# Strassen's seven products for the second matmul, one batch behind, with the attention of batch 1 inside the first stream

## The chip, the cores and the metric

The kernel runs on one core of a Trainium2 chip. Times are microseconds (us) on the device, the median of several executions; each execution is put in a state by its time and by the clock granted to TensorE, and only runs of the fast state are compared. All runs quoted here were of the fast state. PE is TensorE (the matmul engine), PEld its weight loads, PSUM the memory in which its matmuls accumulate, DVE is VectorE, ACT is ScalarE, POOL is GpSimd, SP is SyncE, which here issues transfers.

## The reference, cut to what matters

```
B, H, S, D = 8, 12, 448, 64
scores = q @ k.T / sqrt(64) - log(448)          # per batch and head
x = sigmoid(scores) @ v                         # heads side by side: [3584, 768]
h = x @ w_in                                    # [3584, 2048], the "first GEMM"
out = (h * sigmoid(h)) @ w_out                  # [3584, 768],  the "second GEMM"
```

Inputs and output are 32-bit floats; the kernel multiplies in 16 bits.

## The kernel before

A batch has 448 rows, which are 7 blocks of 64. Matmuls use the array in quarters: four of 64x64 run at once. The kernel is a stream: for each batch 8 pairs of column tiles of the first GEMM, then the output tiles of the second, and between them steps of the next batch's attention (21 per batch: one score with its sigmoid, and one piece of the values). An output tile is two blocks of rows by 768 columns:

```python
def o_pair(units):                      # units: (tile, column half), two of them
    ...
    yield from products(
        "o", NFC, lhs,                  # NFC = 16 slices of 128 of the inner size 2048
        lambda u, k: w_out_sb[:, k, units[u][1] * NO2 : (units[u][1] + 1) * NO2],
        lambda u: po[:, u, :NO2],       # NO2 = 384
    )
    ... # one or two evictions on VectorE with a scale, and the stores

def tiles_of(b):                        # 3 or 4 output tiles after the pairs of batch b
    return range((R * b) // 2, (R * (b + 1)) // 2)
```

Queries and keys come in by rows and have to be transposed. Of batch 1 the second and third thirds of the heads are transposed on PE, inside the stream of batch 0; later batches use DMA transposes:

```python
for kind, share, b in stream:
    ...
    if kind == "h":                                 # a pair of the first GEMM
        if share == 0.5:
            attend()
        if b == 0 and pairs in (2, 5) and 0.9 < share < 1:
            i = 1 if pairs == 2 else 2
            transpose_pe(1, i, "qk", pool=ps_sc, tag="pssc")
            if i == 1:
                cast(1, 2, "q", nc.vector)
                cast(1, 2, "k", nc.gpsimd)
```

The stream of batch 0 ends with three output tiles, so attention of batch 1 is spread over pairs and tiles.

## Time and profile before

The time is 392.29 us (392.22 to 394.06). I cut the execution at the first matmul of the first GEMM of each batch, as PE's timeline shows it; "tail" is batch 7 to the end of the span.

| stretch of the kernel before | us |
|---|---|
| prologue (loads, attention of batch 0) | 28.13 |
| stage 0 | 46.69 |
| stage 1 | 49.27 |
| stages 2 to 6 together | 222.98 |
| tail | 43.31 |
| span | 390.38 |

PE is busy 98% of the span and runs at its peak rate in the steady stages; the lines that carry this are in the prediction (the 2.4 GHz in it is that of the formula of the page that it cites under (1)).

### The profile page before, as it was taken

The numbers are of one execution on the slowest core, as the hardware profiler recorded it, in microseconds if no ns is written. First come the engines' busy times: TensorE is split into PE (matmuls) and PEld (weight loads), VectorE is DVE, ScalarE is ACT, GpSimd is POOL, SyncE is SP. The second block draws the span as 40 slices with busy tenths as digits, with TensorE's granted clock in tenths as the row PEclk, the third lists the DMA queues.
The fourth block names the chain that finished last, engine by engine and source line by source line (L and its number), as shares of the span: only waits on it lengthen the run. The fifth ranks groups of instructions, "written<-read, shape, count | busy, mean of one in ns | idle before, by whom it ended". The sixth has DMA issues, their size and how long they took to land.

```text
span 390.4 us, 16893 instructions
## 1 busy us (share of the span) xinstructions
PE 381.4 (98%) x7944; PEld 296.8 (76%) x7944; DVE 135.2 (35%) x142; ACT 226.7 (58%) x234; POOL 55.2 (14%) x69
## 2 busy tenths in 40 slices
PE   8999999999999999999999999999999999999995
PEld 4665688788888777877788777877788777877785
DVE  3443542234222442144322333234420433324312
ACT  3986576566644776567644777667745677633200
POOL 4622102120300111013100121002100000000000
PEclk9999999999999999999999999999999999999999
DMA  8999997999993767687572875667673100130033
GB/s 289 231 241 243 179 180 158 177 235 251 228 158 64 202 131 161 113 202 150 144 119 54 208 144 143 125 122 202 151 118 83 44 3 2 44 83 1 2 83 82
DMA packets 64998, 54.18 MB, mean 139 GB/s; under 512 B 35488, under 2 KB 61472, under 8 KB 64928
## 3 DMA queue, kind: packets, MB, share of 16 engines
q1 hardware_dynamic: 50768, 40.64, 44.0%
q0 software_dynamic: 13632, 11.80, 20.2%
q8 instruction: 62, 1.02, 1.1%
q10 hardware_dynamic: 528, 0.66, 0.6%
q14 instruction: 8, 0.07, 0.0%
HBM read 45.61 MB, written 11.01 MB: 145 GB/s over the span
## 4 chain that ended last, share of the span: by engine, by line
PE 90%; DMA 6%; DVE 1%; issue 1%; POOL 1%; ACT 0%; SPq 0%; POOLq 0%
DMA v_1_461<-in_v_dram 4%; DMA stk_0_219<-in_k_dram 2%; PE po_0_2_1_1696 L236 1%; PE po_0_24_1_8966 L258 1%; PE po_0_3_1_2401 L236 1%; PE po_0_5_1_2758 L236 1%; PE po_0_12_1_5062 L236 1%; PE po_0_26_1_9104 L258 1%; PE po_0_25_1_9035 L258 1%; PE po_0_23_1_8578 L236 1%; PE po_0_22_1_8391 L236 1%; PE po_0_17_1_7009 L236 1%; PE po_0_8_1_3813 L236 1%; PE po_0_20_1_7531 L236 1%; PE po_0_19_1_7366 L236 1%; PE po_0_18_1_7192 L236 1%
## 5 line engine op out<-in xcount | busy, mean ns | idle before, releaser
L236 PEld LDWEIGHTS <-w_in_sb 64*64 64x64 f16 x2688 | 95.6, 107 | 32.7 <-ACTq L249 7.9
L236 PEld LDWEIGHTS <-gT_712 64*64 64x64 f16 x448 | 18.8, 107 | 3.0 <-issue 0.2
L236 PEld LDWEIGHTS <-gT_5400 64*64 64x64 f16 x448 | 18.2, 107 | 3.4 <-ACTq L249 0.2
L236 PEld LDWEIGHTS <-gT_3096 64*64 64x64 f16 x448 | 18.2, 107 | 3.4 <-ACTq L249 0.2
L236 PEld LDWEIGHTS <-gT_1877 64*64 64x64 f16 x448 | 18.5, 107 | 1.6 <-ACTq L249 0.5
L236 PEld LDWEIGHTS <-gT_6485 64*64 64x64 f16 x448 | 17.2, 107 | 2.5 <-ACTq L249 0.5
L236 PEld LDWEIGHTS <-gT_4181 64*64 64x64 f16 x448 | 17.2, 107 | 2.5 <-ACTq L249 0.5
L258 PEld LDWEIGHTS <-w_in_sb 128*64 128x64 f16 x192 | 12.5, 110 | 5.8 <-issue 0.3
L236 PEld LDWEIGHTS <-gT_7700 64*64 64x64 f16 x384 | 13.7, 107 | 2.5 <-ACTq L249 0.2
L258 PEld LDWEIGHTS <-gT_8740 128*64 128x64 f16 x160 | 12.4, 110 | 1.6
L92 PEld LDWEIGHTS <-zeros 64*64 64x64 f16 x192 | 6.6, 120 | 5.2 <-issue 2.2
L236 PE MATMUL po_0_1_0_1293<-w_out_sb,gT_712 64*64 64x384 f16 x128 | 6.5, 323 | 0.0
L236 PE MATMUL po_0_3_1_2401<-w_out_sb,gT_712 64*64 64x384 f16 x64 | 6.4, 323 | 0.0
L236 PE MATMUL po_0_3_1_2401<-w_out_sb,gT_1877 64*64 64x384 f16 x64 | 6.4, 323 | 0.0
L236 PE MATMUL po_0_21_1_8206<-w_out_sb,gT_7700 64*64 64x384 f16 x128 | 6.4, 323 | 0.0
L236 PE MATMUL po_0_7_1_3620<-w_out_sb,gT_3096 64*64 64x384 f16 x128 | 6.4, 323 | 0.0
L236 PE MATMUL po_0_14_1_5924<-w_out_sb,gT_5400 64*64 64x384 f16 x128 | 6.4, 323 | 0.0
L236 PE MATMUL po_0_2_1_1696<-w_out_sb,gT_712 64*64 64x384 f16 x128 | 6.3, 324 | 0.0
L236 PE MATMUL po_0_15_1_6117<-w_out_sb,gT_5400 64*64 64x384 f16 x128 | 6.2, 323 | 0.0
L236 PE MATMUL po_1_1_1_1480<-w_out_sb,gT_712 64*64 64x384 f16 x128 | 6.2, 323 | 0.0
L236 PE MATMUL po_0_8_1_3813<-w_out_sb,gT_3096 64*64 64x384 f16 x128 | 6.2, 323 | 0.0
L236 PE MATMUL po_0_22_1_8391<-w_out_sb,gT_7700 64*64 64x384 f16 x128 | 6.2, 323 | 0.0
(783 smaller groups left out, 934.2 us busy)
## 6 DMA issues: line engine op xcount, KB each, us to landing
w_in_sb<-in_moe_w_in_dram POOLq DMA_DIRECT2D x8, 384.0 KB, 10.5
w_out_sb<-in_moe_w_out_dram POOLq DMA_DIRECT2D x2, 1536.0 KB, 17.1
v_0_142<-in_v_dram POOLq DMA_DIRECT2D x3, 224.0 KB, 6.1
v_1_461<-in_v_dram POOLq DMA_DIRECT2D x1, 672.0 KB, 14.0
v_2_1551<-in_v_dram POOLq DMA_DIRECT2D x1, 672.0 KB, 9.1
v_3_2037<-in_v_dram POOLq DMA_DIRECT2D x1, 672.0 KB, 8.4
v_4_3256<-in_v_dram POOLq DMA_DIRECT2D x1, 672.0 KB, 6.8
v_5_4341<-in_v_dram POOLq DMA_DIRECT2D x1, 672.0 KB, 6.3
```

The costliest lines, as they stand in the source:

```text
L92: nc.tensor.matmul(pz[half(t), j, :S], zeros[half(j), :D], zeros[half(j)], start=True, stop=True)
L236: mm = nc.tensor.matmul(out_of(u)[half(c)], lhs(u, k, c)[half(row)], rhs(u, k)[half(row)], start=(ph == 0 and k == 0), stop=(ph == 1 and k ...
L258: nc.tensor.matmul(out_of(u)[half(c)], lhs(u, k, c), rhs(u, k), start=(k == 0), stop=(k == nk - 1),)
```

## The change

Intent: fewer matmuls. Eight blocks of rows are taken together as a 2x2 arrangement (two halves of rows, two halves of the inner size), the output weights as 2x2 too, and Strassen's method makes the four result quarters from seven products instead of eight. Its sums of activations and weights go to VectorE. As 56 blocks are seven groups of eight, the second GEMM starts only after batch 1's pairs and runs one batch behind; stage 0 has no output tile left, and all of batch 1's attention lies within its eight pairs and behind them. The diff, cut to its core:

```diff
-            if b == 0 and pairs in (2, 5) and 0.9 < share < 1:
-                ...                      # batch 1's transposes on PE, in the stream
-                transpose_pe(1, i, "qk", pool=ps_sc, tag="pssc")
...
+    for nm in "qk":                      # end of the prologue, behind the loads of batch 1
+        transpose_dma(1, 1, nm)
...
+            if n == 1:                   # n: step of batch 1's attention
+                load_w_in(3)
+                load_v(1)                # the load of it in the prologue stays as well
+            if n == 3:
+                cast(1, 2, "q", nc.vector)
+                cast(1, 2, "k", nc.gpsimd)
+                for nm in "qk":
+                    transpose_dma(1, 2, nm)
+            if n == 14:
+                load_v(2)
+                load_w_out()             # was at steps 4 and 6
...
-            gs = list(tiles_of(b))
-            ... # 3 or 4 tiles of o_pair
+                if b == 1 and f2 >= 4:
+                    sum_w(f2 - 4)        # half a sum of the output weights
+            if b > 0:
+                for s in o_group(b):
+                    yield *s, b
...
+    def o_group(b):                      # x, y: two accumulators in PSUM
+        sum_g(1)
+        ...                              # for batch 1 two half sums of weights, two more below
+        yield from mm(x, of_g(0, 0), w11)
+        p1 = keep(x, "p1", "part1")
+        sum_g(2)
+        yield from mm(y, of_g(0, 1), w21)
+        halves(y, osb[0][:, :, lo], p1)
+        sum_g(4)
+        yield from mm(x, of_s(2), t_sums[2], start=False)   # adds to the product that was kept
+        u2 = keep(x, "u2", "part1")
+        sum_g(3)
+        yield from mm(y, of_s(1), t_sums[1])
+        p5 = keep(y, "p5", "part2")
+        yield from mm(x, of_s(3), t_sums[3], start=False)
+        halves(x, osb[1][:, :, hi], p5)
+        yield from mm(y, of_s(4), w22, start=False)
+        halves(y, osb[0][:, :, hi], u2)
+        yield from mm(x, of_g(1, 1), t_sums[4], start=False)
+        halves(x, osb[1][:, :, lo])
+        ...                              # the stores, here and between the products
```

## The prediction

> **What bounds the kernel now.** I read the page first (busy shares, slices), then the chain of work that ended last, then the timeline of PE at the borders of the stages, then the waits, the timelines of ACT and POOL and the DMA issues.
>
> Page, parts 1 and 2:
>
> ```profile
> PE 381.4 (98%) x7944; PEld 296.8 (76%) x7944; DVE 135.2 (35%) x142; ACT 226.7 (58%) x234; POOL 55.2 (14%) x69
> ...
> PE   8999999999999999999999999999999999999995
> ...
> DMA  8999997999993767687572875667673100130033
> ```
>
> PE has work all the time, no other engine is near its limit over the whole, but the DMA engines are full for the first 13 slices of 9.76 us. A busy PE is not yet a PE at its peak, so I looked at the rate, in the chain in order of time:
>
> ```profile
> 18.69 14.00 DMA v_1_461<-in_v_dram
> ...
> 129.63 1.14 PE ph_2_3220 L236 x24
> ...
> 157.16 1.30 PE po_0_8_1_3813 L236 x32
> ...
> 370.83 5.20 PE po_0_25_1_9035 L258 x64
> ```
>
> 24 matmuls of 64x64x448 take 1.14 us (47.4 ns each), 32 of 64x64x384 take 1.30 us (40.6 ns each), 64 of the full-height form take 5.20 us (81 ns). With four quadrants working at once 448 columns at 2.4 GHz are 46.7 ns: the PE runs at its peak. So in the steady part time is the number of matmuls. Where the stages lie (the first matmul of the first GEMM of batches 0, 1, 2, 3, 6, 7), in the timeline of PE:
>
> ```profile
> 28.13 0.95 PE L236 MATMUL ph_0_713<-xT_414,w_in_sb 64*64 64x448 f16 x16
> ...
> 74.82 1.01 PE L236 MATMUL ph_0_1878<-xT_1262,w_in_sb 64*64 64x448 f16 x16
> ...
> 124.09 0.97 PE L236 MATMUL ph_0_3097<-xT_2367,w_in_sb 64*64 64x448 f16 x16
> ...
> 166.84 0.95 PE L236 MATMUL ph_0_4182<-xT_3586,w_in_sb 64*64 64x448 f16 x16
> ...
> 304.39 0.95 PE L236 MATMUL ph_0_7701<-xT_6975,w_in_sb 64*64 64x448 f16 x16
> ...
> 347.07 0.38 PE L258 MATMUL ph_0_8741<-xT_8176,w_in_sb 128*64 128x448 f16 x2
> ```
>
> So: prologue 28.1, stage 0 46.7, stage 1 49.3, stages 2 to 6 together 223.0 (alternately 42.7 and 47.4, for three or four output tiles), tail 43.3; in all 390.4, and the measured time is 1.9 above the span.
>
> **What the Trainium skill says.** (1) "TensorE: Matmul & The Clock Gate", section "Back-to-back issue gap": about N/2.4 + 2.5 ns per warm matmul. The trace agrees: 81 ns for two column tiles of 384, half of 162.5. (2) "VectorE: DVE Perf Modes", "The perf-mode tier table": tensor_tensor on 16-bit SBUF operands runs at 2x (1224 ns for 2048 elements), at 1x with a PSUM operand. The trace has only PSUM forms: 896 elements in 1.09 us. (3) "PSUM — Partial Sum Buffer", "The four PSUM rules": a matmul without the first flag accumulates, and reads by VectorE don't change that; so the change may read a partial sum, store it and go on adding. No run yet shows it. (4) "DMA: Bandwidth & Descriptors", "Queues, rings and completion order": each DMA engine takes turns between queues packet by packet, so 256-byte packets of a transpose beside 1 KB packets of a load get a small share of the bytes. The trace agrees in part (rivals, below).
>
> **The change part by part.**
> *Removed from PE.* The second GEMM now makes seven products of (4 blocks of 64 rows) x 1024 x 384 for every 8 blocks, where eight were made. Before: 24 tiles of 128 quarter matmuls and the equal of 4 tiles at the end (5.20 us each); after: six groups of 448 and a last one of 7 x 32 full-height ones. 384 x 40.6 ns = 15.6 us, and 20.8 - 18.2 = 2.6 us in the tail: 18.2 us. The four PE transposes of batch 1 (56 short matmuls, about 2.3 us seen as longer pairs 2 and 5 of stage 0) become DMA transposes.
> *Where it falls.* A stage of batches 1 to 6 now has 8 row blocks for the work of 7, so it isn't shorter than before: 8 pairs of the first GEMM at 2.65 (one attention step in each) = 21.2; 448 x 40.6 ns = 18.2; 13 attention steps x 8 x 47.4 ns = 4.9; allowance for hand-overs 0.5; sum 44.8, against a mean of 44.6 before. The gain is that stage 0 loses its three output tiles (15.6 us) and stage 1 and the tail half a tile each.
> *Added to DVE.* Per group four sums of 2048 elements, about 1.2 us each by (2), and seven evictions where 3.5 were, 0.95 us each:
>
> ```profile
> 370.87 0.96 DVE L305 TENSOR_SCALAR osb_8965<-po_0_24_1_8966 128x768 f32<-128x768 f32 x1 [3.21 <-PE po_0_24_1_8966 L258]
> ```
>
> About 8 us more per group, 56 us in all, and 8 sums of weights (7 us once). Inside a group a product with its two attention steps takes 64 x 40.6 + 2 x 379 = 3.36 us, and DVE has one eviction, one sum and at times an eviction of attention, 2.2 to 3.2 us. It keeps up. Critical is product 3: its sum waits for the eviction of product 1, 0.2 + 0.95 + 1.2 = 2.35 us after product 1's end, and product 2 covers 3.36. So on the path nothing, but in the tail, without attention, a product takes 2.6 us and DVE also about 2.6 (its sums are split in two there): I allow 1.2 us of stalls.
> *Row change-overs.* The order of instructions shows 14 instead of 7 per two batches. They cost nothing where an attention step lies between the halves, and the new places (every 8 steps) are such.
> *Stage 0.* Its 21 scores now all have to lie within eight pairs. PE: two scores and 48 matmuls = 2.65, with less attention to cover the row change-over: 2.8. ACT needs two score sigmoids at a spacing of 0.89 and one of the GEMM:
>
> ```profile
> 24.46 1.05 ACT L191 ACTIVATE attnT_2_520<-psc_2_4_614,bias_s 128x896 f16<-128x896 f32 x1
> 25.35 1.06 ACT L191 ACTIVATE attnT_2_520<-psc_2_5_633,bias_s 128x896 f16<-128x896 f32 x1
> ```
>
> 2.6 us, just below. So 8 x 2.8 + 0.3 = 22.7. Then four scores, all 21 value steps and the next batch's first score, 26 pieces of 4 matmuls at 0.19 us = 4.9; and the value accumulator has one buffer, so it waits for its eviction twice (1.3 each), 0.7 for a PSUM slot that the seventh pair's multiply frees, 0.4 at the end: 8.6. With a wait for the transposes of 5.5 (first rival): 36.8.
> *Sum.* 28.1 + 36.8 + stage 1 (44.8 + 1.8 for the arrival of the output weights and the sums of weights) 46.6 + 5 x 44.8 = 224.0 + tail (18.4 + 18.2 + 1.2 + 4.2 from the last matmul to the end, 3.9 before) 42.0 = 377.5; plus 1.9 = 379.4 us, 3.3% below.
>
> **Rivals.**
> *A. Stage 0 waits for DMA.* The order of instructions shows that batch 1's values are loaded twice (the old load stays, and a second one is added behind the last input weights), and that the transposes of its second third of heads stand in their queue behind the load of its last third:
>
> ```profile
> 37.50 0.93 POOL L148 CAST xk_2_929<-stk_2_653 128x896 f16<-128x896 f32 x1 [7.26 <-DMA stk_2_653<-in_k_dram]
> ...
> stk_2_653<-in_k_dram SPq DMA_DIRECT2D x1, 448.0 KB, 10.5
> ...
> w_out_sb<-in_moe_w_out_dram POOLq DMA_DIRECT2D x2, 1536.0 KB, 17.1
> ```
>
> That load lands at 37.4, the transposes come behind it while the weights and the second value load (0.69 MB at about 0.19 MB per us, estimate 3.6 us) keep the engines full until about 44. Scores need them at about 38. Later in the trace a transpose alone moves 204 GB/s (last column), and the next one, as a value load sets in beside it, far less:
>
> ```profile
> 64.00:65.00 1.00, 1.00 (x29) 0.74 (x24) 0.57 (x1) 0.49 (x2) 0.63 (x1) 1.00 1.05 204
> 65.00:66.00 1.00, 1.00 (x34) 0.89 (x28) 0.00 (x0) 0.81 (x1) 0.00 (x0) 1.00 0.67 39
> ```
>
> So the wait is 0 to 9 us; I took 5.5. Without it the time is 374; at 9, 383.
> *B. The output weights come late.* They are asked for near the end of stage 0 instead of at 38 us, need 17 us alone, and share the engines with batch 2's loads. The sums of weights are wanted about 22 to 25 us later and stand in DVE's order before multiplies that free PSUM. For: the same 0.19 MB per us. Against: two pairs of slack. It would make 379 into 382 to 385.
> *C. DVE becomes the bound inside the groups* (sums at 1x, 2.2 us each, or held up by casts on POOL). A product would then be 3.5 to 4.3 us instead of 3.36: 7 x 7 x 0.5 = 25 us, all gain gone, 395 or more. Against: the skill's table and a DVE share of about 52%. I give it 5%.
>
> **Range and chances.** Steady stages are well known (each 0.3 us there makes 1.5 us); stage 0's wait has a width of 9 us, stage 1's 4, the tail's 2. That gives 373 to 386. The limit of 2% is 384.5, reached only if A and B are both bad, or by C: faster 0.82, within 0.16, slower 0.02.
>
> **What would show it.** Stage borders in PE's timeline: stages 2 to 6 at 44.8 each (over 46 says C), stage 0 at 36.8 (31 says that no wait for transposes happened), tail 42.0. Sums of 2048 elements at 1.2 us. The waits of PE list the scores of batch 1 behind a DMA, and DVE's first sum of weights behind the output weights. Matmuls fall by 504. Wrong would be: PE idle inside the groups behind DVE, or a stage 0 that takes no time for transposes.

## The result, and the profile after

The changed kernel takes 387.56 us (386.62 to 389.35, 4 runs) against 392.43 of the kernel before in the same rounds: ratio 0.9872, 95% interval 0.9825 to 0.992, which at the 2% limit is "same". The time lies above the predicted range. (Ratios here are the mean time of one kernel's fast runs over that of the other's of the same rounds, so not quite the ratio of the medians that I quote.)

The page after: PE's busy time and matmuls, then PE, PE's clock and DMA in 40 slices, here of 9.66 us:

```profile
PE 360.9 (93%) x7440; PEld 272.8 (71%) x7440; DVE 195.4 (51%) x213; ACT 225.6 (58%) x234; POOL 58.9 (15%) x70
...
PE   7999079799899999999999999999999999999995
...
PEclk9999669999999999999999999999999999999999
DMA  8999968999999959199642975568760600032005
```

There are 504 matmuls fewer, as intended, and PE is busy 20.5 us less. But slice 5 (38.6 to 48.3 us) has PE at 0, and there and in the next slice the clock is at six tenths. Before, no slice of PE was below 8 except the last, and the clock row was all nines. The first matmuls of batches 0, 1, 2 and 7 in PE's timeline (start, duration, then what it is):

```profile
28.58 0.39 PE L251 MATMUL ph_0_741<-xT_428,w_in_sb 64*64 64x448 f16 x4
...
74.44 0.39 PE L251 MATMUL ph_0_1464<-xT_1369,w_in_sb 64*64 64x448 f16 x4
...
122.07 0.35 PE L251 MATMUL ph_0_2663<-xT_1970,w_in_sb 64*64 64x448 f16 x1
...
345.06 0.38 PE L275 MATMUL ph_0_8554<-xT_7892,w_in_sb 128*64 128x448 f16 x2
```

| stretch | before | predicted | after | miss |
|---|---|---|---|---|
| prologue | 28.13 | 28.1 | 28.58 | +0.5 |
| stage 0 | 46.69 | 36.8 | 45.86 | **+9.1** |
| stage 1 | 49.27 | 46.6 | 47.64 | +1.0 |
| stages 2 to 6 | 222.98 | 224.0 | 222.99 | -1.0 |
| tail | 43.31 | 42.0 | 41.41 | -0.6 |
| span | 390.38 | 377.5 | 386.48 | +9.0 |

The whole miss is stage 0. In the view of waits, the longest of PE, and in the chain of work that ended last, in order of time, what stands around it:

```profile
PE psc_1_0_981 L197 <- DMA kT_1_701<-xk_1_631: 11.7, 1, 11.7
```

```profile
31.62 19.20 DMA kT_1_701<-xk_1_631
50.82 0.04 issue
50.87 0.59 PE psc_1_0_981 L197 x3
51.45 2.24 PE ph_3_954 L251 x18
53.69 0.40 PE psc_1_1_1012 L197 x3
```

kT_1 is the transposed keys of batch 1's second third. Their transfer is issued at 31.62 and lands at 50.82; the first score that reads them waits 11.7 us. After it PE is slow. Table by windows (width, busy time of PE, PEld, DVE, ACT, POOL with counts, the granted clock, DMA share, GB/s):

```profile
41.50:42.00 0.50, 0.00 (x0) 0.00 (x0) 0.00 (x0) 0.00 (x0) 0.00 (x0) 1.00 0.24 16
...
42.50:43.00 0.50, 0.00 (x0) 0.00 (x0) 0.00 (x0) 0.00 (x0) 0.00 (x0) 0.50 1.23 198
...
55.00:55.50 0.50, 0.50 (x12) 0.31 (x8) 0.00 (x0) 0.50 (x2) 0.00 (x0) 0.50 0.00 0
...
56.00:57.00 1.00, 1.00 (x28) 0.53 (x24) 1.00 (x1) 0.69 (x1) 0.00 (x0) 1.00 0.64 82
```

PE stops at 39.2; at 42 the clock falls to half, and it comes back only between 55.5 and 56, some 5 us after PE has started again. The Trainium skill, "TensorE: Matmul & The Clock Gate", section "What's actually happening", puts the fall to half after an idle window of about 3.4 us and the return after about 3.4 us of sustained work, with a window that runs freely, so that the moment varies by 0.5 us. The trace has 2.8 us and about 4.8 us; other kernels of this study spread more widely (closing list).

Why is the transfer late? The DMA view of three stretches: the software queue carries the loads issued by POOL, the hardware queue those issued by SP, the transposes among them (packets, MB, share). First the changed kernel from 37.4, when batch 1's last load has landed, to 51:

```profile
q0 software_dynamic: 1654, 1.54, 74.3%
q1 hardware_dynamic: 2723, 0.67, 54.6%
```

then, within it, from 38 to 42 and from 42 to 46:

```profile
q0 software_dynamic: 466, 0.46, 90.4%
q1 hardware_dynamic: 474, 0.12, 46.8%
```

```profile
q0 software_dynamic: 644, 0.60, 89.2%
q1 hardware_dynamic: 638, 0.16, 30.3%
```

and from 50.9 to 51.9, after the software queue has run dry:

```profile
q1 hardware_dynamic: 910, 0.22, 116.0%
```

While both have work the two queues advance packet for packet (466 and 474, 644 and 638), though a load's packet is about 1 KB and a transpose's 256 bytes. Four transposes wait in the queue, 896 packets each; the keys are the second, so 1792 packets have to pass. From 38 to 46 they pass at 139 per us (1112 in 8 us), alone at 910. About 1.1 of these 8 us are a stall of both queues, from 41.0 to 42.1 (the table above has 16 GB/s at 41.5 and 198 at 42.5); by their packets experiments 2, 4, 5, 10 and 12 have one too, between 40 and 43, and its cause is open. Outside it the transposes pass at about 150 to 170 per us. This is the turn-taking that the prediction quoted from the skill, seen here in counts. It slows the loads as well: outside the stall they move 0.15 MB per us, where the prediction reckoned with 0.19.

### The profile page after: what moved, and what is told of

It is laid out like the page before. It is cut to its first block, busy times and chain, and to the rows that moved or that the text cites. A ratio compares the mean times of both kernels' runs of the same rounds, so it can differ in the third digit from the quotient of the medians.

```text
span 386.5 us, 16052 instructions
## 1 busy us (share of the span) xinstructions
PE 360.9 (93%) x7440; PEld 272.8 (71%) x7440; DVE 195.4 (51%) x213; ACT 225.6 (58%) x234; POOL 58.9 (15%) x70
## 3 DMA queue, kind: packets, MB, share of 16 engines
q10 hardware_dynamic: 768, 1.25, 0.9%
## 4 chain that ended last, share of the span: by engine, by line
PE 73%; DMA 15%; DVE 6%; ACT 4%; issue 1%; SPq 0%; POOL 0%; DVEq 0%; POOLq 0%
DMA w_out_sb<-in_moe_w_out_dram 7%; DMA kT_1_701<-xk_1_631 5%; PE po_2_3194 L251 3%; PE po_6_7923 L251 3%; PE po_3_4382 L251 3%; PE po_4_5570 L251 3%; PE po_5_6756 L251 3%; PE po_1_2002 L251 2%; PE po_5_6757 L251 2%; PE po_4_5571 L251 2%; PE po_2_3195 L251 2%; PE po_3_4383 L251 2%; PE po_6_7924 L251 2%; DMA stk_0_1019<-in_k_dram 1%; PE po_7_8780 L275 1%; DMA stq_0_90<-in_q_dram 1%
## 5 line engine op out<-in xcount | busy, mean ns | idle before, releaser
L251 PEld LDWEIGHTS <-w_in_sb 64*64 64x64 f16 x2688 | 92.7, 108 | 39.1 <-ACTq L266 9.7
L197 PE MATMUL psc_1_0_981<-qT_1_699,kT_1_701 64*64 64x448 f16 x4 | 0.6, 578 | 11.7 <-DMA kT_1_701<-xk_1_631 11.7
L251 PEld LDWEIGHTS <-gT_6224 64*64 64x64 f16 x160 | 9.6, 107 | 0.9 <-ACTq L266 0.2
L197 PEld LDWEIGHTS <-kT_1_701 64*64 64x64 f16 x28 | 0.9, 119 | 12.7 <-DMA kT_1_701<-xk_1_631 12.1
L251 PEld LDWEIGHTS <-gT_2662 64*64 64x64 f16 x176 | 8.7, 107 | 0.6 <-ACTq L266 0.5
L251 PEld LDWEIGHTS <-gT_1463 64*64 64x64 f16 x176 | 8.1, 107 | 1.1 <-ACTq L266 0.3
L295 DVE TENSOR_TENSOR gT_740<-ph_3_954,tsig_3_1022 128x896 f16<-128x896 f32 x1 | 1.1, 1091 | 14.9 <-ACT tsig_3_1022 L294 14.9
L251 PEld LDWEIGHTS <-gT_3850 64*64 64x64 f16 x176 | 7.0, 107 | 1.1 <-ACTq L266 0.5
L201 ACT ACTIVATE attnT_1_0_980<-psc_1_0_981,bias_s 128x896 f16<-128x896 f32 x1 | 1.0, 1007 | 11.5 <-PE psc_1_0_981 L197 11.5
L251 PEld LDWEIGHTS <-gT_740 64*64 64x64 f16 x176 | 6.9, 107 | 1.1 <-ACTq L266 0.3
L251 PEld LDWEIGHTS <-gT_5038 64*64 64x64 f16 x160 | 6.7, 107 | 1.4 <-ACTq L266 0.5
L251 PEld LDWEIGHTS <-gT_7409 64*64 64x64 f16 x128 | 6.1, 107 | 1.0 <-ACTq L266 0.5
L275 PEld LDWEIGHTS <-gT_8553 128*64 128x64 f16 x80 | 5.9, 110 | 1.1
L216 PEld LDWEIGHTS <-v_1_776 64*64 64x64 f16 x84 | 3.0, 106 | 3.8 <-issue 2.9
L112 POOL DMA_DIRECT2D w_in_sb<-in_moe_w_in_dram x8 | 5.3, 674 | 0.0
L102 PE MATMUL pz_start<-zeros 64*64 64x448 f16 x44 | 3.9, 531 | 1.2 <-DVE bias_s L80 1.2
L216 PEld LDWEIGHTS <-v_2_1235 64*64 64x64 f16 x84 | 3.3, 107 | 1.5 <-issue 1.0
L251 PE MATMUL po_1_2002<-t_1787,s_1_2107 64*64 64x384 f16 x64 | 3.0, 324 | 1.4 <-DVE s_1_2107 L349 1.4
L201 ACT ACTIVATE attnT_0_0_204<-psc_0_0_205,bias_s 128x896 f16<-128x896 f32 x1 | 1.0, 1007 | 5.4 <-PE psc_0_0_205 L197 5.4
L216 PEld LDWEIGHTS <-v_4_2821 64*64 64x64 f16 x84 | 3.9, 107 | 0.3
```

What stands on the lines that cost most here:

```text
L102: nc.tensor.matmul(pz[half(t), j, :S], zeros[half(j), :D], zeros[half(j)], start=True, stop=True)
L112: nc.gpsimd.dma_start(w_in_sb[half(t), :, f], moe_w_in[t * NCC * D : (t + 1) * NCC * D, f].rearrange("(c d) f -> d c f", d=D),)
L197: nc.tensor.matmul(psc[half(j), t, :S], kT[half(t), r, half(j)], qT[half(t), :, half(j)], start=True, stop=True,)
L201: return nc.scalar.activation(attn[b, i, r], psc[:, :, :S], AF.Sigmoid, bias=bias_s, scale=QKSCALE)
L216: nc.tensor.matmul(pav[half(t), j, :S], v16s[b][half(j), t, i, r * D : (r + 1) * D], attnT[half(j), t, :], start=(r == 0), stop=(r == R - 1),)
L251: mm = nc.tensor.matmul(out_of(u)[half(c)], lhs(u, k, c)[half(row)], rhs(u, k)[half(row)], start=(start and ph == 0 and k == 0), stop=(ph ...
```

## Experiments

Each experiment is the changed kernel with the edit shown. Stage 0 and the pairs are measured as above. "Pair" is one of the eight pairs of the first GEMM.

### 1. Batch 1's transposes back on PE

```diff
-    for nm in "qk":
-        transpose_dma(1, 1, nm)
...
-                for nm in "qk":
-                    transpose_dma(1, 2, nm)
...
+        if pairs in (2, 5) and 0.9 < share < 1:
+            transpose_pe(1, 1 if pairs == 2 else 2, "qk", pool=ps_v)
+            ...                          # and the casts of the last third, moved here
```

> The changed kernel, but the transposes of batch 1's second and third thirds of heads go to PE (as in the kernel before), none to DMA. Theory (stage 0 loses its gain to the wait for the DMA transpose, 11.7 us, and to the halved clock after it): the wait and the slow clock go, about 14 us; PE gets back 56 short matmuls, about 2 us, and the scores may wait 1 us for DVE's copies. Stage 0 from 45.9 to about 33, time from 387.6 to about 375. Rival (the wait is only moved: the output weights or the values arrive late anyway and stage 1 takes it): stage 0 shrinks, stage 1 grows by as much, time stays within 3 us of 387.

Measured: 379.55 us (378.11 to 380.29), ratio to before 0.9679 (0.9643 to 0.9715), faster. Stage 0 is 35.72 instead of 45.86, with the 56 short matmuls that the transposes put back on PE. The clock row is all nines. Expected were about 33 and 375, so the gain came smaller than forecast. The DMA transposes had cost stage 0 ten us, although they took work off PE. Stage 1 became 49.2 (+1.6): batch 2's first keys were waited for 1.0 us, and the group of batch 1, with its sums of weights, took 26.1 us where later groups take 23.3.

### 2. The second load of batch 1's values left out

```diff
                 load_w_in(3)
-                load_v(1)
```

> The changed kernel without the second load of batch 1's values. Theory of contention (the transposes share each DMA engine packet by packet with the loads of weights and values, and are done when those run dry): 0.69 MB less in the other queue, at 0.15 to 0.19 MB per us 3.6 to 4.6 us, so kT lands at about 46 to 47 instead of 50.8, wait 7 to 8 us instead of 11.7, time about 383. Rival (the transposes wait only for their place behind the key load in their own queue, or for their own packets): kT lands at 50 to 51 as before, time 387.

Measured: 385.3 us (384.34 to 386.84), ratio 0.9834. The wait:

```profile
PE psc L197 <- DMA kT<-xk: 9.5, 1, 9.5
```

With 672 KB less in the software queue the keys land 2.0 us sooner, at 48.83, and the wait is 2.2 us shorter. Counted in the trace, the first 1792 packets of transposes have passed at about 46.2 us instead of 48.2; in both the landing follows 2.6 us later. The direction is that of contention, the size about half of what I expected: until about 45 us the transposes take turns with the input weights, which stay. One trace is thin evidence for the size: experiment 5 has the same transfers in stage 0 as the changed kernel, and there the keys land at 48.17 and are waited for 8.4 us. Nor do the times decide, as the intervals of the two ratios overlap.

### 3. The transposes ahead of the last load of queries and keys

```diff
-            for i2, at in enumerate(((0, 0), (1, 0), (2, 5))):
+            for i2, at in enumerate(((0, 0), (1, 0))):
                 ...
     for nm in "qk":
         transpose_dma(1, 1, nm)
+    stage(1, 2, behind=act)
```

> The changed kernel, but the last load of batch 1's queries and keys (0.9 MB) is put behind the transposes of the second third instead of ahead of them. Theory of contention: the packets of the transposes start at about 29 instead of 35, at 10 packets per engine and us (100 per engine each third) they need about 10 us, so kT lands at 40 to 43 and the wait falls from 11.7 to 2 to 5; but the key load lands later, and so the third third's transposes, which may then be waited for at the 14th score. Time 380 to 385. Rival of the place in the queue: kT lands at about 33 to 35, no wait there, time 376 or less.

Measured: 387.72 us (387.11 to 388.65), ratio 0.9887: no gain, where 380 to 385 was expected. The wait for the keys is nearly gone (0.7 us), but two others have come, in the view of waits:

```profile
PE ph L251 <- DVE gT L295: 9.3, 4, 8.4
...
DVE xq L160 <- DMA stq<-in_q_dram: 16.1, 3, 12.6
```

The load that now stands behind lands late, DVE's cast of it stands in DVE's order before the multiplies that free PE's accumulators, and PE waits 8.4 us for those. The same bytes have to come, and putting one transfer ahead of the other moved the wait to another engine.

### 4. and 12. PE kept busy while it waits

```diff
         if share == 0.5 or share == 1:
+            if s_done == 7:
+                idle(56, "wait")        # 47 in the second version; matmuls on zeros
             attend((ps_sc, ps_v)[s_done % 2])
```

> The changed kernel with 56 groups of four matmuls of zeros (10.6 us at full clock) put in front of the score that waits for the transpose. Theory: the wait itself stays (kT lands at 50.8), but PE's clock isn't halved when it comes back; the two halves of a pair after the wait took 2.4 us instead of 1.3 and the third too, so the time falls by 2 to 3 us, to about 385. Rival (the slow pairs after the wait are due to ACT or PSUM, not the clock): no change.

Measured with 56: 388.28 us (387.38 to 390.41), ratio 0.9907. The clock stays at 1.0, but the idle matmuls end at 51.9, about 1.4 us after the keys land (50.5). From the waiting score to the end of the fifth pair it is 4.75 us instead of 6.67, so the halved clock had cost 1.9 us there; the time doesn't show it, as the overrun took it back. Hence the shorter version, which was the last run of the study:

> As the fourth experiment, with 47 instead of 56 idle groups of matmuls ahead of the waiting score, so that they should end near 50 us, before the transposed keys land at 50.8 in the change's trace. Theory (halved clock after the wait costs 1.9 us): the clock stays at 1.0, the stretch from the score to the next pair takes 4.75 us as in the fourth experiment instead of 6.67, and the time is 385.5 to 386.3. Rival (the halved clock costs nothing on the path, ScalarE or the next wait hides it): 387.6 like the change. In the fourth experiment the two could not be told apart by the time, as its idle groups ran past the landing.

Measured with 47: 386.85 us (386.31 to 389.21, 6 runs), ratio 0.9881 (0.9856 to 0.9906). In the profiled run the fourth and fifth pairs together take 17.4 us instead of 19.7, 2.3 less. But batch 2's first keys are now waited for too (2.2 us), the clock halves after that wait, from 74.65 to 78.07, and the profiled execution, the slowest of the six, gives all of it back:

```profile
PE psc L197 <- DMA kT<-xk: 3.4, 2, 2.2
```

So the cost of the clock in stage 0 is shown in the trace, at 1.9 to 2.3 us; that removing it alone makes the kernel faster is not shown: 387.6 was the rival's number, and 386.85 lies between the two.

### 5. Strassen undone, the rest of the change kept

The group makes eight plain products with the same operands, accumulators and order of attention; no sums.

```diff
-        sum_g(1)
-        ... # the seven products
+        for row in range(2):
+            yield from mm(x, of_g(row, 0), w11)
+            yield from mm(y, of_g(row, 0), w12)
+            yield from mm(x, of_g(row, 1), w21, start=False)
+            halves(x, osb[row][:, :, lo])
+            yield from mm(y, of_g(row, 1), w22, start=False)
+            halves(y, osb[row][:, :, hi])
...                                      # all sums of weights go; stores as before
+                elif o_steps > 12 * NK2:
+                    pass                 # no attention step in and behind the seventh product
```

> The changed kernel with Strassen undone alone: the same eight-block groups one batch behind, the same stage 0 and loads, but eight plain products of 2.6 us per group (two accumulated per output), four evictions, no sums. If Strassen gives what its count says: one product more per group, 6 x 64 x 40.6 ns + 2.6 us = 18.2 us, less 1 to 2 us of DVE waits and weight sums that also go: time about 387.6 + 17 = 404 to 405, and stages 2 to 6 grow from 44.6 to 47.2. Rival (DVE's sums and evictions eat part of it inside the groups): stages grow by clearly less than 2.6, time under 400.

Measured: 407.21 us (406.2 to 409.26), ratio 1.0403, that is 19.7 us over the changed kernel. Groups in the steady stages take 26.24 us instead of 23.31, the last one 21.00 instead of 18.91. Strassen by itself is worth about what the matmuls said. Two things blur the figure: a steady group is 2.93 us longer and not the 2.6 of one product, perhaps because the seventh product now has no attention step between its halves; and stage 0, which the edit doesn't touch, came out 3.0 us shorter in this trace. The other half of the change, the eight blocks one batch behind, without Strassen is 4% slower than the kernel before.

### 6. and 7. Three repairs at once, and the same with Strassen undone

PE transposes as in 1, one load of values as in 2, and the output weights asked for at the eighth score of batch 1 instead of the fifteenth:

```diff
+            if n == 7:
+                load_w_out()
             if n == 14:
                 load_v(2)
-                load_w_out()
```

> Three repairs together: transposes of batch 1 on PE, one load of batch 1's values (the later one), and the output weights asked for at the 7th score instead of the 14th. Theory (stages 0 and 1 are bound by the order of early transfers, the rest by PE): stage 0 about 35, stage 1 from 49.2 (with PE transposes alone) to 46 to 47 because the sums of weights no longer wait; time 376 to 377. Rival (the transfers only change places: batch 2's queries and keys then come late beside the output weights): stage 1 gets a wait for a transpose of 2 us or more, time 379 or above.

Measured: 386.58 us (385.53 to 387.97), ratio 0.9872: as slow as the change itself. The repairs 1 and 2 are in it, so the early weights cost some 8 us. The wait is the old one, one batch later:

```profile
PE psc L197 <- DMA kT<-xk: 5.9, 1, 5.9
```

The transposed keys of batch 2 are issued at 55.95 beside the weights and land at 69.49, 13.5 us later, and the clock halves once more. Moving 3 MB forward put them beside the next transposes.

> The repaired kernel with Strassen undone. Theory: 18 us above the repaired one, so about 394, that is the kernel before within 1%: all of the gain is Strassen's, and the move of batch 1's attention and of the groups gives none. Rival (the rearrangement has a worth of its own): below 388.

Measured: 404.26 us (402.45 to 405.77), ratio 1.0319; 17.7 us over the kernel with Strassen of the same rounds, with groups of 26.24 against 23.31. Together with experiment 5: 17.7 and 19.7 measured, 18.2 predicted.

### 8. Each sum of activations made twice

The second one writes the same values, so the result stays right. Base: the kernel of experiment 6.

```diff
                 if x == 1:
-                    nc.vector.tensor_add(o, part(1, 0, i0, i1), part(1, 1, i0, i1))
+                    for _ in range(2):
+                        nc.vector.tensor_add(o, part(1, 0, i0, i1), part(1, 1, i0, i1))
                 ... # the other three alike
```

> The repaired kernel with each of DVE's sums of activations made twice, 4 x 1.2 us more of DVE per group. Theory (a product with its two attention steps takes 3.36 us and DVE has 2.2 to 3.2 in it; the third product's operand is ready 1 us early): doubled sums use up that slack and overrun it by about 0.2 to 1.5 us at products 3 and 5, so 0.5 to 3 us per attending group and 3 to 5 us in the tail: 7 to 20 us more. If DVE had been on the path already, the whole 7 x 4.8 = 34 us would appear; if it had ample slack, under 3 us.

Measured: 417.25 us (415.61 to 418.45), ratio 1.0639, 30.7 us over its base. Groups in the steady stages take 26.4 to 28.5 us, 3.0 to 5.2 more, and the group of batch 1 8.5 more, for 4 x 1.2 = 4.8 us of added DVE time. (The clock halved twice after waits of the doubled kernel, in the groups of batches 1 and 3, which is part of the largest figures.) PE now waits where it did not before:

```profile
PE po L251 <- DVE s L351: 16.4, 7, 6.4
PE pav L216 <- DVE xT L228: 9.8, 9, 1.3
```

My expectation of 7 to 20 was wrong; it is close to the 34 of a DVE that is already on the path. In the changed kernel itself PE hardly waits for DVE in a group (once 1.4 us, in the group of batch 1 with its sums of weights), so VectorE does keep up, but with a margin of 2 us per group at most. The trace of the changed kernel shows where it is thin. In batch 3's group DVE is busy 14.1 of 23.3 us, but most of its idle time comes behind the sums. The second sum ends at 193.56, and the third product, which reads it, starts at 194.75: the margin is 1.2 us there, close to the 1.0 that the prediction had worked out. The page's 51% for DVE doesn't tell that: it is an average over pairs and groups.

### 9. PE transposes and one load of values

Experiments 1 and 2 together; the output weights stay at the fifteenth score.

> Batch 1's second and third thirds transposed on PE as in the first experiment, and the second load of batch 1's values (672 KB) left out; the output weights stay where the change asks for them. Theory (what is left of stage 0's and stage 1's excess is DMA that comes late): the loads behind the dropped one land about 2 us sooner, so the 1.0 us wait for batch 2's first transposed keys goes and DVE's 2.1 us wait for the output weights too: stage 1 falls from 49.2 to 47 to 48, time 377.5 to 379. Rival (the excess is DVE's order alone): 379.5 as before.

Measured: 378.34 us (377.5 to 379.91, 6 runs), ratio to before 0.9641 (0.9601 to 0.9681): faster than both kernels, and the lowest time of this study (the intervals of this ratio and of experiment 1's overlap, so the second load's own worth is not shown). PE's slices have no hole:

```profile
PE   7999997999999999999999999999999999999995
```

Stage 0 is 34.89, and no wait of PE for a DMA is left in the stream. Stage 1 is 48.4, not the 47 to 48 that I expected: the group of batch 1 takes 25.8 us, 2.5 over a steady one. That group has four sums of weights on DVE besides (0.94 us each), which is more than the margin seen in experiment 8.

### 10. Meant: no load of values ahead of the transposes

```diff
-                if i == 1:
-                    load_v(1)            # in the prologue
...
                 load_w_in(3)
-                load_v(1)
+            if n == 8:
+                load_v(1)
```

> The change as it is, its DMA transposes kept, but neither load of batch 1's values stands before them any more: the first is left out, the second is asked for at the ninth score of batch 1, after the wait. Theory (the transposes wait because the loads' queue keeps the DMA engines busy): each 672 KB that leaves the stretch brings the transposed keys forward by 2 us or more, as the one of the second experiment did (9.5 from 11.7): wait 5 to 7.5 us, the halved clock shorter, time 381 to 384, unless the values now come late. Rival (the transposes are slow in themselves, 19 us whatever runs beside them): wait 9.5 to 11.7, time 385 to 388.

Measured: 386.18 us (385.04 to 386.6), ratio 0.9832. The edit doesn't do what I meant. The load is in POOL's order behind its last cast and did not wait for the score:

```profile
33.14 0.84 POOL L147 DMA_DIRECT2D v<-in_v_dram  x1
```

So the load that was to come after the wait goes out sooner than the second load of the changed kernel (35.02), and more than half of its packets move before the keys have landed. This kernel has one load in the stretch, as experiment 2 has, only the other one; a kernel with neither was not run. The keys, issued at 29.20, land at 46.94 instead of 50.82:

```profile
PE psc L197 <- DMA kT<-xk: 9.4, 2, 7.7
```

The longest wait is 7.7 instead of 11.7, and 9.5 in experiment 2 with as many bytes. The keys come sooner than in any trace with both loads, which is the direction of contention; how much 672 KB costs is not shown. The other wait, 1.7 us, is for keys of batch 2. Stage 0 is 41.71; the time expected (381 to 384) was missed, as stage 1 grew to 49.3.

### 11. Weights early, and batch 2's first third transposed on PE as well

As experiment 9, with the weights at the eighth score, and:

```diff
+                        if (b, i2) != (1, 0):
                             transpose_dma(b + 1, i2, nm)
...
     attend_v(2 * R)
+    transpose_pe(2, 0, "qk", pool=next_slot())
     attend_v(N1)
```

> As the first kernel of this call, and the output weights asked for at batch 1's eighth score (as in the sixth experiment), with the first third of batch 2 transposed on PE too, so that no DMA transpose is wanted while the weights load. Theory (the 5.9 us wait of the sixth experiment was the same wait, moved to batch 2's keys): that wait is gone, no wait for the output weights, 1.1 us of PE more: time 376 to 378.5. Rival (the wait moves on once more, to batch 2's second third, or its loads come late): 380 to 385.

Measured: 385.3 us (382.19 to 385.57), ratio 0.9802: a miss. The profiled execution was the fastest of the six (382.19), so 3 us of the median are not in this trace. In it PE waits for no DMA, but I had put the transposes where they delay what follows. The end of stage 0 in the chain, in order of time:

```profile
63.71 0.62 DVE qT L183
64.34 0.54 DVE kT L183
64.92 0.41 PE psc L197 x4
...
65.42 1.01 ACT attnT L201
66.43 0.82 ACT tsig L294
67.27 1.10 DVE gT L295
68.42 2.45 PE ph L251 x24
```

The score of batch 2 waits for DVE's two copies; its sigmoid stands in ACT's order before that of the last pair, whose multiply on DVE frees the accumulator for batch 1's first pair. Half of that pair, 24 matmuls, then takes 2.45 us, about twice its usual 1.3: the clock had halved again, from 67.82 to 71.23. Whether early weights would help with a better place for these transposes stays open; stage 1 was 47.6 here against 48.4, so there is at most about 1 us in it.

## Why the prediction was wrong

**The step that failed is the size of stage 0's wait for the transposes.** The prediction named the mechanism as rival A (the transposes stand behind a load and share the DMA engines with weights and the second load of values) and gave it "0 to 9 us; I took 5.5". Measured: 11.7 us of wait, and about 1.9 us more of halved clock after it. 13.6 - 5.5 = 8.1 of the 9.1 us missed in stage 0; the other 1.0 is within the rest of that stage's sum (without wait and clock 32.3 against 31.3 predicted). Experiments 1 and 9 show that it is the transposes: with them on PE the times are 379.55 and 378.34. (That this is near the predicted 379.4 is partly chance: these kernels have no wait of 5.5 us, but 56 matmuls more.)

Three terms of that estimate were wrong. It let the load queue run dry at about 44, 6.6 us after 37.4, which at 0.19 MB per us is 1.25 MB; the trace has 1.54 MB from 37.4 on. 0.19 was read from stretches with loads alone; beside transposes it was 0.15, since the queues alternate packet for packet. And the loads did not run evenly: there was the stall, and the last 0.17 MB took from 47.5 to 50.6. 1.54 / 0.19 = 8.1 us, 1.54 / 0.15 = 10.3 us, and the last of it went out 13.2 us after 37.4: of the 6.6 us that were missing, 1.5 are the amount, 2.2 the rate and 2.9 the stall and the slow end. The prediction had cited the rule of taking turns, used it only for the transposes, and forgot that it slows the loads by the same packets. It also had no term for the clock, though the page that it cites for TensorE has the clock gate in its title.

Three of its readings do not hold, though none moves the forecast by much. The line from 65 to 66 us (39 GB/s) is not a transpose beside a load: by their packets one transpose had ended at 65.3, the next began at 66.6, and the value load was only starting. From 67 to 68 the two do run together, 138 packets of the transpose to 161 of the load. The DMA engines were full for the first 12 slices, not 13 (the 13th is a 3). And the page of citation (1) gives its formula for an isolated matmul and says that it over-counts in a stream with many columns; the 81 ns of this stream fit the formula all the same.

**Rival B, late output weights:** right in kind and small. The sum of weights waited 0.9 us for them:

```profile
L315 DVE TENSOR_TENSOR t_1788<-w_out_sb 128x1536 f16<-128x1536 f16 x2 | 2.7, 1334 | 0.9 <-DMA w_out_sb<-in_moe_w_out_dram 0.9
```

Stage 1 was 1.0 us over the sum. Experiment 6 shows that asking for them earlier, beside batch 2's transposes, is no cure; experiment 11 leaves open whether it helps without these. Most of stage 1's excess over a steady stage is in batch 1's group (25.7 us instead of 23.3), where PE waits 1.4 us for a sum of activations that stands behind sums of weights in DVE's order.

**Rival C, DVE as the bound:** it did not happen, as predicted. The sums took the predicted 1.2 us (in the group's lines: busy, mean ns):

```profile
L349 DVE TENSOR_TENSOR s_1_2107<-s_1_2004,gT_740 128x2048 f16<-128x2048 f16 x1 | 1.2, 1207 | 0.0
```

The 5% given to it rested on that rate, which held. The margin behind it is thin: sums at half the rate are what experiment 8 made, and there PE waited for them and the time rose by 30.7 us.

**Matmuls removed:** right. 504 fewer, 56 of them transposes; 18.2 us predicted for the other 448, 17.7 and 19.7 measured by undoing Strassen in two settings. **Steady stages:** right, 222.99 against 224.0; a product with its attention took 3.36 us as worked out. **Tail:** 41.41 against 42.0; PE waited for DVE once, 0.2 us, where 1.2 were allowed. **Partial sums in PSUM:** all kernels that read an accumulator and went on adding to it gave correct results.

Where did the gain go, then? Strassen's 18 us were there. Part of them pays for the new order of the stream: with all of its waits repaired, the order costs about 4 us (estimate from experiments 9 and 7: 378.3 + 17.7 = 396.0 without Strassen, against 392). The other 9 us, 387.6 - 378.3, were lost to transfers that share the DMA engines with others.

## What to carry to other kernels

Replacing a few us of transposes on a busy PE by a DMA transfer is a gain only if the transfer lands before it is needed, and beside a load that takes far longer: here its small packets advanced at the load's packet rate, and both became slower. Look in the trace, too, whether a load that was moved in the program really goes out later: POOL's did not in experiment 10. For a transfer that a score waits for, count the packets in all queues from issue to need, and set that against the time; then add the halved clock: here it followed waits from about 2 us on (closing list). And when a repaired wait gives no gain, look one batch further for the same wait before giving up: here it came back as a cast in DVE's order, as batch 2's keys, and as a sigmoid in ACT's order.

## What the Trainium skill lacked or had wrong

- "DMA: Bandwidth & Descriptors", "Queues, rings and completion order": the turn-taking by packets is right (644 to 638 packets in 4 us), but no page gives a figure for what a queue of small packets loses by it beside a load, or for what the load loses. Here transposes fell from 910 packets per us alone to about 150 to 170, and the loads from 0.19 to 0.15 MB per us.
- "TensorE: Matmul & The Clock Gate", "What's actually happening": it lets the moment vary by 0.5 us around about 3.4 us. Here the spread is wider: in the nine waits during which the clock fell, it fell 2.5 to 4.3 us after PE stopped and was back 2.8 to 4.9 us after PE started. Waits of 1.9, 1.9 and 2.2 us (experiments 3, 8 and 12) were followed by a halved clock within 1.1 us of PE's start, while two of 2.6 and 2.7 us in experiment 8 were not. The free-running window of the page fits: every halved stretch inside the stream lasted 3.41, 6.83, 10.24 or 13.65 us, which are multiples of 3.41.
- "VectorE: DVE Perf Modes", "The perf-mode tier table": agrees for whole sums of 2048 elements (1207 to 1225 ns in eleven of thirteen, 1269 and 1410 in the others). No page says how a margin of VectorE inside a stretch is to be told; its share of the span doesn't tell it (30.7 us for doubled sums at a share of 51%, experiment 8), the time from the end of a sum to its reader does (1.2 us).
